# The last five output products of a fused attention and two-MLP kernel, by seven products of 256 columns

## The chip, the core and the metric

One core of a Trainium2 chip runs the whole program. The metric is the device time of one execution in microseconds, as a median of runs. The matrix engine is TensorE (PE in the rows, PEld for its weight loads), the vector engine VectorE (DVE), the scalar engine ScalarE (ACT); SP issues nearly all DMAs.

## The reference: what is computed

A linear attention with a normalisation gives x of 2304 tokens by 512; a first MLP with a gate follows, and then the second block, to which the change belongs:

```python
a = x @ w_a          # (2304, 512) @ (512, 1536)
b = x @ w_b          # (2304, 512) @ (512, 1536)
return (a * b @ w_out).astype(np.float32)   # (2304, 1536) @ (1536, 512)
```

## The kernel before

The matrices are kept as pairs of float32r, a high part and a low part (value minus high), and each product is three matmuls: high by high, high by low, low by high.

The tokens form six blocks of 384, and two blocks make a pair d (0, 1, 2). The 1536 hidden columns form six pairs p of 2 x 128. A *step* n (0 to 17) is one d and one p; in the middle pair of blocks (steps 6 to 11) p runs backwards. In a step TensorE computes *half a* (a = x @ w_a, transposed) and *half b*, and then the *output product of the step before*, as `out_mm(n - 1)` stands behind `products(n)` in the loop. The output of step 17 comes last.

Both halves use a seven-product scheme (function `seven`, L691 for its matmuls): two blocks by two hidden blocks, seven products of sums instead of eight plain ones. Products go to four PSUM banks X, Y, V, X, Z, V, Z; a bank that comes twice is accumulated into after its first value was read. u2 is ScalarE's copy of the first product, completed by an add (L698) behind the second; u3 is an add behind the third (L701). Then the four results A11, A22, A12, A21 (block of tokens, hidden half) fall out behind the products 3 to 6, counted from 0, of half a by a copy (L730) and adds (L732), of half b by an add (L745) and a product with a's result (L742, L746). Each result gets a high part on ScalarE (L748) and a low part on VectorE (L752), in a page `ab`.

The output product `out_mm` takes, for two blocks and three groups of 128 tokens, six matmuls of 512 columns (L885) into one of four PSUM banks of the tag `acc`, and adds the bank to the accumulator in SBUF (L893); the first step of a pair of blocks copies it on ScalarE (L891), the last one also stores it.

The weights' parts (`wa`, `wb` as seven operands, `w_out` as two tiles) lie in DRAM (`wd`, nine tiles of 512 KB per p) and are loaded by `load_pairs` (L652) as far ahead as 21 live tiles allow. They share 37 pages of SBUF with the parts of `ab`, the accumulators and temporary tiles. At the turn from one pair of blocks to the next the tiles of two p's stay (`KEPT`). In steps 7 to 10 sums of the next pair's x are made on ScalarE and VectorE between the output adds (`combine`, L437, L438, L491), and stored.

The order on each engine is the order in which the code issues instructions. An engine executes its queue in that order.

Of the kernel before, what the change touches and what calls it, by code (L numbers as in the profile page):

```python
# [15 lines left out]
P = 128  # L16
# [44 lines left out]
def tile_linattn_moe_moe2(ctx: ExitStack, tc: tile.TileContext, q, k, v, g_norm,  # L61
# [25 lines left out]
    had = dr.tile([NF1 // 2, P, 3 * DM], F32, tag="had", name="had")  # L87
    hsd = dr.tile([NF1 // 2, 2, P, 2 * DM], F32, tag="hsd", name="hsd")
    xcd = dr.tile([NB // 2, 7, P, 2, 2, TB], F32, tag="xcd", name="xcd")
    wd = dr.tile([NF2 // 2, 9, P, 2 * DM], F32, tag="wd", name="wd")  # L90
    first = tc.alloc_tile_pool(name="first", bufs=1)

    def page(shape, dt, name):
        return sb.tile(shape, dt, tag="page", bufs=NPAGE, name=name)
# [534 lines left out]
    NPAIR = NF2 // 2  # L629
    seq = [(d, p) for d in range(NB // 2) for p in (range(NPAIR) if d % 2 == 0 else reversed(range(NPAIR)))]  # L630
    live, wanted = [(0, False)] * 7, []
    for n, (d, p) in enumerate(seq):
        if n >= NPAIR and n % NPAIR < KEPT:
            continue
        end = n
        if d + 1 < NB // 2 and n % NPAIR >= NPAIR - KEPT:
            end = (d + 1) * NPAIR + NPAIR - 1 - n % NPAIR
        order = tuple(range(9)) if n >= NPAIR else (7, 8) + (tuple(range(7)) if n else ())
        wanted.extend((p, i, end) for i in order)

    def load_pairs(most=NLIVE):
        for _ in range(most):
            if not wanted or len(live) >= NLIVE:
                return
            p, i, end = wanted.pop(0)
            live.append((end, i >= 7))
            if len(w2raw) < NF2 and i >= 7:
                load_w(("w2", 2 * p + i - 7))
                w2raw.append((p, i - 7))
                continue  # L650
            t = page([P, 2 * DM], F32R, f"wp_{p}_{i}")
            nc.sync.dma_start(t.bitcast(F32), wd[p, i])  # L652
            wp[p, i] = t

    def free_pairs(n, last):

        live[:] = [e for e in live if e[0] > n or e[1] != last]
# [54 lines left out]
    def seven_ab(d, p, mat, place):  # L712
        return seven(f"{'ab'[mat]}_{d}_{p}", lambda name, wq, kt: w_part(p, mat, name, wq, kt),
                     lambda i, xq, kt: xc[d, i][:, xq, kt, :],
                     lambda nm: sb.tile([P, TB], F32, tag=place, bufs=PLACES[place], name=nm))

    PLACES = {"mid": 5, "sig": 2, "gh": 2, "gl": 2}
    ab = {}

    def products(d, p, after=None, more=()):  # L720

        a = {}
        for n, got in enumerate(seven_ab(d, p, 0, "mid")):
            if n == 2 and after is not None:
                after()
            if got is not None:
                f, i, z, u = got
                t = a[f, i] = sb.tile([P, TB], F32, tag="mid", bufs=5, name=f"a_{d}_{p}_{f}{i}")
                if u is None:
                    nc.scalar.copy(t, z)  # L730
                else:
                    nc.vector.tensor_add(t, z, u)  # L732
            if 1 <= n <= len(more):
                more[n - 1]()
        low = None
        for n, got in enumerate(seven_ab(d, p, 1, "sig")):
            if got is None:
                continue
            f, i, z, u = got
            t = a[f, i]  # L740
            if u is None:
                nc.vector.tensor_mul(t, z, t)  # L742
            else:
                c = sb.tile([P, TB], F32, tag=("gh", "gl")[f], bufs=2, name=f"b_{d}_{p}_{f}{i}")
                nc.vector.tensor_add(c, z, u)  # L745
                nc.vector.tensor_mul(t, c, t)  # L746
            o = page([P, 2, TB], F32R, f"ab_{d}_{p}_{f}{i}")
            nc.scalar.copy(o[:, 0], t)  # L748

            if low:  # L750
                low()
            low = lambda t=t, o=o: nc.vector.tensor_sub(o[:, 1], t, o[:, 0].bitcast(F32))  # L752
            ab[d, p, f, i] = o
        low()

    whole_ = {}

# [111 lines left out]
    def rows(j, t):  # L869
# [2 lines left out]
            return blk.rearrange("(p c) m -> p c m", c=CH)[:, t]  # L872
        return blk[t * P:(t + 1) * P]

    def out_mm(n, more=()):

        d, p = seq[n]
        first_, last_ = n % NPAIR == 0, n % NPAIR == NPAIR - 1
        for n in range(2):
            for i in range(CH):  # L880
                c = n * CH + i
                ts = slice(i * P, (i + 1) * P)
                o = ps.tile([P, DM], F32, tag="acc", bufs=4, name=f"op_{d}_{p}_{c}")
                for k, (f, g, wq) in enumerate([(f, g, wq) for f in range(2) for g, wq in ((0, 0), (0, 1), (1, 0))]):
                    nc.tensor.matmul(o, ab[d, p, f, n][:, g, ts], wp[p, 7 + f][:, wq * DM:(wq + 1) * DM],  # L885
                                     start=(k == 0), stop=(k == 5))
                if first_ and c % 2 == 0:
                    oacc[d, c // 2] = page([P, 2, DM], F32, f"o_{d}_{c}")
                t = oacc[d, c // 2][:, c % 2]
                if first_:  # L890
                    nc.scalar.copy(t, o)  # L891
                else:
                    nc.vector.tensor_add(t, o, t)  # L893
                if last_:
                    nc.sync.dma_start(rows(2 * d + n, i), t)
                for f in more[c] if c < len(more) else ():
                    f()
        for f in range(2):
            for n in range(2):
                ab.pop((d, p, f, n))  # L900


    w1 = [(kind, f) for f in range(NF1) for kind in ("wi", "wo")]
# [337 lines left out]
    with tc.manual_schedule():  # L1241
# [61 lines left out]
            x1s = [(vi, NF1 - 1)]  # L1303
        prev = 8, NF1 - 1
        todo, late = [], {}
        for n, (d, p) in enumerate(seq):
            new = 0 < n < NPAIR
            m = n % NPAIR
            if 1 <= m <= 4 and n < 2 * NPAIR:

                kt, h = divmod(m - 1, 2)
                if h == 0:
                    late[kt] = combine(d + 1, kt, late.pop("blocks"))
                todo = late[kt][6 * h:6 * h + 6]
            products(d, p, (lambda: x1_mm(*prev)) if n == 0 else None,
                     decode_out(p, 0) if 0 < n < NPAIR else [])
            if n % NPAIR == NPAIR - 1 and n + 1 < len(seq):
                for i in range(7):
                    load_x(d + 1, i)
            free_pairs(n, False)  # L1320
            load_pairs()
            if n > 0:
                more = [(f,) for f in decode_out(p, 1)] if new else []
                if todo:
                    more = [(tuple(more[i]) if more else ()) + tuple(todo[i]) for i in range(6)]
                out_mm(n - 1, more)
                todo = []
                free_pairs(n - 1, True)
                load_pairs()
            if n < 2 * NPAIR and m in (0, 2):  # L1330
                late["blocks"] = last_blocks(d + 1, m // 2)
            put()
# [32 lines left out]
```

## Time and profile before

| | us |
|---|---|
| median of 3 runs | 864.08 (863.89 to 864.09) |
| the profiled execution | 864.65 |
| its span | 862.9 |
| TensorE, VectorE, ScalarE busy | 852.0, 621.1, 347.2 |
| a step of the last pair of blocks | 22.79 |

The span runs from the first to the last instruction; the rest of the execution's time lies around it. Step 6 begins at 577.46, step 12 at 714.26, step 17 at 828.20, the output product of step 17 at 851.0. A row of the timeline gives the start from the span's begin, the time to the end of its last instruction, engine, line, operation, tiles (out<-in), shapes and how many instructions it merges; in brackets the idle time of the engine before it and what ended it. Matmuls overlap, so the distance of starts is what one costs.

### The profile page before, as it was taken

What the parts mean: (1) busy time and instruction counts of PE and PEld (TensorE: products, weight loads), DVE (VectorE), ACT (ScalarE), POOL (GpSimd) and SP (SyncE); (2) the same over time, 40 slices, a digit from 0 to 9 for tenths busy, and PEclk for the clock granted to TensorE, in tenths of its full rate; (3) what the DMA queues carried; (4) which work ended last, traced back from release to release, by engine and by line L of the source; (5) the groups of instructions that cost most, each with busy time, mean ns of one, the idle gap of its engine ahead of it and who ended that gap; (6) DMA issues with size and microseconds to landing.
All of it is one profiled execution on the core that took longest, in us unless ns stands there. A gap on an engine that the chain in (4) does not pass through costs nothing. (4 is left out here: it accounts for less than half of the span.)

```text
span 862.9 us, 13632 instructions
## 1 busy us (share of the span) xinstructions
PE 852.0 (99%) x4966; PEld 807.0 (94%) x4967; DVE 621.1 (72%) x1191; ACT 347.2 (40%) x708; POOL 52.7 (6%) x73
## 2 busy tenths in 40 slices
PE   8999999999999999999999999999999999999998
PEld 5799999999999999999999999999999999999996
DVE  4879979777946879797766788876576665535555
ACT  4667765544535556555532533221412211121110
POOL 5430211000000400000000000000000000000000
PEclk9999999999999999999999999999999999999999
DMA  9995876289986659998899888496788475755001
GB/s 285 356 265 166 230 241 211 92 313 405 402 298 186 207 213 372 407 394 314 314 417 416 321 331 335 147 372 236 255 291 287 141 283 205 293 220 195 1 0 74
DMA packets 126147, 226.35 MB, mean 262 GB/s; under 512 B 40704, under 2 KB 86272, under 8 KB 126080
## 3 DMA queue, kind: packets, MB, share of 16 engines
q1 hardware_dynamic: 126080, 225.48, 72.7%
q8 instruction: 39, 0.64, 0.3%
q14 instruction: 28, 0.23, 0.1%
HBM read 156.50 MB, written 68.94 MB: 261 GB/s over the span
## 5 line engine op out<-in xcount | busy, mean ns | idle before, releaser
L380 PE MATMUL x1p<-gh,wo 128*128 128x384 f32 x768 | 194.9, 337 | 0.0
L380 PEld LDWEIGHTS x1p<-gh,wo 128*128 128x128 f32 x768 | 138.0, 188 | 0.3 <-ACT gh L364 0.3
L380 PE MATMUL x1p<-gl,wo 128*128 128x384 f32 x384 | 128.4, 338 | 0.8 <-DVE gl L369 0.8
L885 PE MATMUL op<-wp,ab 128*128 128x512 f32 x360 | 83.4, 390 | 0.0
L748 ACT CAST ab<-a 128x384 fp32r<-128x384 f32 x72 | 37.0, 514 | 115.1 <-DVE a L742 58.2
L885 PEld LDWEIGHTS op<-wp,ab 128*128 128x128 f32 x360 | 67.5, 188 | 13.7
L369 DVE TENSOR_TENSOR gl<-g,gh 128x384 fp32r<-128x384 f32 x96 | 54.0, 564 | 31.6 <-ACT gh L364 31.3
L380 PEld LDWEIGHTS x1p<-gl,wo 128*128 128x128 f32 x384 | 71.9, 188 | 2.8 <-DVE gl L369 2.6
L893 DVE TENSOR_TENSOR o<-op,o 128x512 f32<-128x512 f32 x90 | 60.3, 684 | 16.7 <-PE op L885 16.7
L885 PE MATMUL op<-w,ab 128*128 128x512 f32 x288 | 66.9, 390 | 0.0
L885 PEld LDWEIGHTS op<-w,ab 128*128 128x128 f32 x288 | 54.0, 188 | 10.9
L364 ACT CAST gh<-g 128x384 fp32r<-128x384 f32 x96 | 49.1, 512 | 21.9 <-PE x1p L380 18.6
L354 PE MATMUL hp<-xh,wi 128*128 128x384 f32 x256 | 52.7, 345 | 0.4 <-ACT xh L260 0.3
L238 POOL TENSOR_TENSOR rr<-ss,nhalf 128x6 f32<-128x6 f32 x24 | 34.4, 1435 | 229.8 <-DVE ss L233 229.8
L354 PEld LDWEIGHTS hp<-xh,wi 128*128 128x128 f32 x256 | 43.8, 188 | 1.4 <-ACT xh L260 1.0
L691 PE MATMUL Z_a<-xc,wp 128*128 128x384 f32 x216 | 43.4, 335 | 0.1
L691 PE MATMUL Z_b<-xc,wp 128*128 128x384 f32 x216 | 43.3, 335 | 0.0
L691 PE MATMUL V_b<-xc,wp 128*128 128x384 f32 x216 | 43.3, 335 | 0.0
L691 PE MATMUL V_a<-xc,wp 128*128 128x384 f32 x216 | 43.3, 335 | 0.0
L752 DVE TENSOR_TENSOR ab<-a,ab 128x384 fp32r<-128x384 f32 x72 | 39.8, 553 | 2.3 <-ACT ab L748 0.8
L691 PE MATMUL X_a<-xc,wp 128*128 128x384 f32 x204 | 41.3, 337 | 0.0
L691 PE MATMUL X_b<-xc,wp 128*128 128x384 f32 x204 | 40.9, 334 | 0.0
(175 smaller groups left out, 1555.2 us busy)
## 6 DMA issues: line engine op xcount, KB each, us to landing
wp<-wd SPq DMA_DIRECT2D x107, 512.0 KB, 6.2
hw<-hsd SPq DMA_DIRECT2D x32, 512.0 KB, 8.3
xc<-xcd SPq DMA_DIRECT2D x21, 768.0 KB, 8.5
hw<-had SPq DMA_DIRECT2D x16, 768.0 KB, 8.4
xcd<-b SPq DMA_DIRECT2D x24, 384.0 KB, 4.5
raw_wi<-in_moe_w_in_dram SPq DMA_DIRECT2D x16, 512.0 KB, 6.6
raw_wo<-in_moe_w_out_dram SPq DMA_DIRECT2D x16, 512.0 KB, 6.2
hsd<-hs SPq DMA_DIRECT2D x16, 512.0 KB, 5.3
```

What stands on the lines that cost most here:

```text
L238: nc.gpsimd.tensor_tensor(r, rms[j, p], nhalf, op=ALU.pow)
L354: nc.tensor.matmul(o, w[wp][:, kt * P:(kt + 1) * P], x[key][:, kt, :], start=(n == 0), stop=(n == 3 * KD - 1))
L364: nc.scalar.copy(gh, src)
L369: nc.vector.tensor_sub(gl, src, gh.bitcast(F32))
L380: nc.tensor.matmul(acc[vi][c], w[wp][:, c * P:(c + 1) * P], gg[vi, s][g], start=(s == s0 and i == 0), stop=(s == s1 - 1 and i == 2))
L691: nc.tensor.matmul(b[bank], w(name, wq, kt), x(i, xq, kt), start=(fresh and k == 0), stop=(k == 5), skip_group_check=True)
L748: nc.scalar.copy(o[:, 0], t)
L752: low = lambda t=t, o=o: nc.vector.tensor_sub(o[:, 1], t, o[:, 0].bitcast(F32))
L885: nc.tensor.matmul(o, ab[d, p, f, n][:, g, ts], wp[p, 7 + f][:, wq * DM:(wq + 1) * DM], start=(k == 0), stop=(k == 5))
L893: nc.vector.tensor_add(t, o, t)
```

## The change

The output products of steps 12 to 16 are made from a 2 x 2 form as well: blocks of tokens by hidden halves on one side, the hidden halves by 256 output columns of `w_out` on the other. Seven products of 256 columns each (three groups of tokens, three matmuls each: 63 matmuls) replace 36 matmuls of 512 columns (`out_seven`). Their partial results are accumulated in two pairs of banks, U and Z, and are read out after each product: 512 columns (two token groups) and 256 columns (the third).

For that, half b of those steps ends in sums: S1 = A21 + A22 behind its last product, and S2, S3, S4 in the next half a, behind its products 1 and 2, with the low parts spread over the products behind; the low parts of S3 and A12 lie in the output product behind its products 1 and 2. A21 itself gets no parts. In steps 12 to 16 the output product of the step before stands between half a and half b, instead of behind b; in step 17 it stands behind b as before.

The sums T1 to T4 of `w_out` are made in half a of steps 8 to 12 (`t_parts`) from the tiles of the step before. The sums of steps 7, 8 and 9 are stored as two more tiles each in `wd` and loaded again; those of steps 10 and 11 stay. From step 6 to step 11 the tiles ahead are limited to 17, then to 21 again, plus the four kept T tiles. The diff, cut:

```diff
+    def by_seven(n):
+        return 2 * NPAIR <= n < 3 * NPAIR - 1
...
         order = tuple(range(9)) if n >= NPAIR else (7, 8) + (tuple(range(7)) if n else ())
+        if by_seven(n):
+            order += 9, 10
...
-    def load_pairs(most=NLIVE):
+    nlive, more_live = [NLIVE], []
+    def load_pairs(most=2 * NLIVE):
         for _ in range(most):
-            if not wanted or len(live) >= NLIVE:
+            if not wanted or len(live) >= nlive[0] + sum(more_live):
...
-                     lambda nm: sb.tile([P, TB], F32, tag=place, bufs=PLACES[place], name=nm))
-
-    PLACES = {"mid": 5, "sig": 2, "gh": 2, "gl": 2}
+                     lambda nm: sb.tile([P, TB], F32, tag=place if isinstance(place, str) else place[nm[:2]],
+                                        bufs=5 if place == "mid" else 2, name=nm))
...
+    def a_half(d, p, after=None, more=(), place="mid"):
 
         a = {}
-        for n, got in enumerate(seven_ab(d, p, 0, "mid")):
+        for n, got in enumerate(seven_ab(d, p, 0, place)):
...
-                more[n - 1]()
-        low = None
+                for fn in more[n - 1]:
+                    fn()
+        return a
...
+    def b_half(d, p, a, sums_too=False):
+        low = {}
+        def high(name, t):
+            o = ab[d, p, name] = page([P, 2, TB], F32R, f"ab_{d}_{p}_{name}")
+            nc.scalar.copy(o[:, 0], t)
+            low[name] = lambda: nc.vector.tensor_sub(o[:, 1], t, o[:, 0].bitcast(F32))
+        st = {}
...
+            name = f"A{i + 1}{f + 1}"
+            st[name] = t
+            if sums_too:
+                if name != "A21":
+                    high(name, t)
+                continue
+            wait = list(low)
+            high(name, t)
+            for e in wait:
+                low.pop(e)()
+        if not sums_too:
+            low.pop("A21")()
+            return [], []
+        def sub(op, to, x, y, tag):
+            t = st[to] = sb.tile([P, TB], F32, tag=tag, bufs=2, name=f"{to}_{d}_{p}")
+            op(t, st[x], st[y])
+            high(to, t)
+        def lo(name):
+            return lambda: low.pop(name)()
+        sub(nc.vector.tensor_add, "S1", "A21", "A22", "gh")
+        return ([(lambda: sub(nc.vector.tensor_sub, "S2", "S1", "A11", "gl"),
+                  lambda: sub(nc.vector.tensor_sub, "S3", "A11", "A21", "sig")),
+                 (lo("S1"), lambda: sub(nc.vector.tensor_sub, "S4", "A12", "S2", "sig")),
+                 (lo("A11"),), (lo("S2"), lo("A22")), (lo("S4"),), ()],
+                {1: lo("S3"), 2: lo("A12")})
...
+    H2 = 2 * P
+    OUT_PRODUCTS = (("A11", "B11", "U", ((0, 0),)), ("S1", "T1", "Z", ((1, 1),)), ("S2", "T2", "U", ((0, 1),)),
+                    ("S4", "B22", "Z", ((0, 1),)), ("S3", "T3", "U", ((1, 1),)), ("A12", "B21", "W", ((0, 0),)),
+                    ("A22", "T4", "U", ((1, 0),)))
...
+    def out_seven(n, more):
+        d, p = seq[n]
+        first_ = n % NPAIR == 0
+        banks_ = {c: [ps.tile([P, 2, H2], F32, tag="acc", bufs=4, name=f"{c}o{i}_{d}_{p}") for i in range(2)]
+                  for c in "UZ"}
+        banks_["W"] = banks_["Z"]
+        begun, done = set(), set()
+        for m, (an, bn, bank, outs) in enumerate(OUT_PRODUCTS):
+            x = ab[d, p, an]
+            if bn[0] == "B":
+                w, c0, step = wp[p, 6 + int(bn[1])], (int(bn[2]) - 1) * H2, DM
+            else:
+                e = int(bn[1]) - 1
+                w, c0, step = wp[p, 9 + e // 2], e % 2 * H2, DM
+            for i in range(CH):
+                o = banks_[bank][i // 2]
+                for k, (xq, wq) in enumerate(((0, 0), (0, 1), (1, 0))):
+                    fresh = (bank, i // 2) not in begun
+                    begun.add((bank, i // 2))
+                    nc.tensor.matmul(o[:, i % 2], x[:, xq, i * P:(i + 1) * P], w[:, wq * step + c0:wq * step + c0 + H2],
+                                     start=fresh, stop=(k == 2), skip_group_check=True)
+                if i == 0:
+                    continue
+                for r, h in outs:
+                    hs = slice(h * H2, (h + 1) * H2)
+                    t, e = o_at(d, r, 0 if i == 1 else 2, first_)
+                    t, z = (t[:, :, hs], o) if i == 1 else (t[:, e, hs], o[:, 0])
+                    if first_ and (r, h, i) not in done:
+                        nc.scalar.copy(t, z)
+                    else:
+                        nc.vector.tensor_add(t, z, t)
+                    done.add((r, h, i))
+            if m in more:
+                more.pop(m)()
...
+    def t_parts(n):
+        d, p = seq[n]
+        keep = n >= 2 * NPAIR - KEPT
+        tmp, o = [], []
+        def whole(f):
+            if f == 0:
+                t = page([P, 2, DM], F32, f"wf_{p}")
+                tmp.extend((t[:, 0], t[:, 1]))
+            w = wp[p, 7 + f].bitcast(F32)
+            nc.vector.tensor_add(tmp[f], w[:, 0:DM], w[:, DM:])
+        def first_two():
+            t = page([P, 4, H2], F32, f"t_{p}")
+            tmp.append(t)
+            nc.vector.tensor_sub(t[:, 0], tmp[0][:, H2:], tmp[0][:, 0:H2])
+            nc.vector.tensor_sub(t[:, 2], tmp[1][:, H2:], tmp[0][:, H2:])
+        def last_two():
+            t = tmp[2]
+            nc.vector.tensor_sub(t[:, 1], tmp[1][:, H2:], t[:, 0])
+            nc.vector.tensor_sub(t[:, 3], tmp[1][:, 0:H2], t[:, 1])
+        def high():
+            for i in range(2):
+                o.append(page([P, 2 * DM], F32R, f"wt_{p}_{i}"))
+                nc.scalar.copy(o[i][:, 0:DM], tmp[2][:, 2 * i:2 * i + 2].rearrange("p i f -> p (i f)"))
+        def low():
+            for i in range(2):
+                nc.vector.tensor_sub(o[i][:, DM:], tmp[2][:, 2 * i:2 * i + 2].rearrange("p i f -> p (i f)"),
+                                     o[i][:, 0:DM].bitcast(F32))
+                if keep:
+                    wp[p, 9 + i] = o[i]
+                    live.append((4 * NPAIR - 1 - n, True))
+                else:
+                    stores.append(lambda i=i: nc.sync.dma_start(wd[p, 9 + i], o[i].bitcast(F32)))
+            if keep:
+                more_live.append(2)
+        return [(lambda: whole(0),), (lambda: whole(1),), (first_two,), (last_two,), (high,), (low,)]
...
+        chain, later = [], {}
+        def out_step(n, more=(), later=()):
+            if by_seven(n):
+                out_seven(n, later)
+            else:
+                out_mm(n, more)
+            free_pairs(n, True)
+            load_pairs()
...
-            products(d, p, (lambda: x1_mm(*prev)) if n == 0 else None,
-                     decode_out(p, 0) if 0 < n < NPAIR else [])
+            more = [(f,) for f in decode_out(p, 0)] if new else chain
+            if NPAIR < n - 1 < 2 * NPAIR:
+                more = t_parts(n - 1)
+            a = a_half(d, p, (lambda: x1_mm(*prev)) if n == 0 else None, more,
+                       {"u2": "gh", "u3": "gl"} if by_seven(n - 1) else "mid")
+            swap = 2 * NPAIR <= n < len(seq) - 1
+            if swap:
+                out_step(n - 1, (), later)
+            for e in sorted(later):
+                later.pop(e)()
+            after_b = b_half(d, p, a, by_seven(n))
+            if swap:
+                chain, later = after_b
+            if n in (NPAIR, 2 * NPAIR - 1):
+                nlive[0] = 17 if n == NPAIR else NLIVE
...
-            if n > 0:
+            if n > 0 and not swap:
                 more = [(f,) for f in decode_out(p, 1)] if new else []
                 if todo:
                     more = [(tuple(more[i]) if more else ()) + tuple(todo[i]) for i in range(6)]
-                out_mm(n - 1, more)
+                out_step(n - 1, more, later)
                 todo = []
-                free_pairs(n - 1, True)
-                load_pairs()
```

## Rows read from the trace of the kernel before

**Rows 1.** The page: busy time (share) and instructions, and the span in 40 slices.
```profile
PE 852.0 (99%) x4966; PEld 807.0 (94%) x4967; DVE 621.1 (72%) x1191; ACT 347.2 (40%) x708; POOL 52.7 (6%) x73
...
PEclk9999999999999999999999999999999999999999
```

**Rows 2.** Timeline of TensorE over step 15: half a's first products, the output product.
```profile
782.62 1.23 PE L691 MATMUL X_a<-xc,wp 128*128 128x384 f32 x6
783.69 1.20 PE L691 MATMUL Y_a<-xc,wp 128*128 128x384 f32 x6
784.73 1.20 PE L691 MATMUL V_a<-xc,wp 128*128 128x384 f32 x6
...
797.21 8.36 PE L885 MATMUL op<-wp,ab 128*128 128x512 f32 x36
```

**Rows 3.** The chain that ended last: start, us on the chain, step.
```profile
797.37 8.20 PE op L885 x36
```

**Rows 4.** Stretches of steps 8, 10, 13, 15: us, PE, PEld, DVE, ACT, POOL, clock, DMA, GB/s.
```profile
623.06:645.86 22.80, 22.80 (x121) 21.36 (x120) 14.34 (x27) 5.42 (x11) 0.00 (x0) 1.00 0.82 291
...
668.66:691.46 22.80, 22.80 (x121) 21.36 (x120) 15.94 (x31) 4.55 (x10) 0.00 (x0) 1.00 0.42 143
...
737.05:759.84 22.79, 22.79 (x122) 21.35 (x121) 10.28 (x19) 6.23 (x12) 0.00 (x0) 1.00 0.68 254
...
782.62:805.41 22.79, 22.79 (x122) 21.35 (x120) 13.46 (x24) 3.50 (x7) 0.00 (x0) 1.00 0.44 162
```

**Rows 5.** Groups by shape: count, busy us, mean ns of one, idle before.
```profile
L885 PEld LDWEIGHTS op<-wp,ab 128*128 128x128 f32 x360 | 67.5, 188 | 13.7
...
L893 DVE TENSOR_TENSOR o<-op,o 128x512 f32<-128x512 f32 x90 | 60.3, 684 | 16.7 <-PE op L885 16.7
...
L791 DVE TENSOR_TENSOR hs<-hs 128x512 fp32r<-128x512 f32 x16 | 10.3, 683 | 0.6 <-ACT hs L787 0.6
...
L256 PE MATMUL xtp<-ident,sq 128*128 128x128 f32 x48 | 7.8, 272 | 0.0
```

**Rows 6.** Timeline of weight loads after a wait: one load, then two, in windows.
```profile
538.02 0.19 PEld L691 LDWEIGHTS Z_a<-xc,wp 128*128 128x128 f32 x1 [0.44 <-DVE a L732]
...
538.02 0.30 PEld L691 LDWEIGHTS Z_a<-xc,wp 128*128 128x128 f32 x2 [0.44 <-DVE a L732]
```

**Rows 7.** Timeline of TensorE: three transposes; the product behind the one that waited.
```profile
304.29 0.49 PE L256 MATMUL xtp<-ident,sq 128*128 128x128 f32 x3
...
539.17 0.51 PE L691 MATMUL X_b<-xc,wp 128*128 128x384 f32 x2
```

**Rows 8.** Timeline of VectorE: two sums of 256 columns; the add that was waited for.
```profile
103.37 0.42 DVE L781 TENSOR_TENSOR hs<-hs,hs 128x256 f32<-128x256 f32 x1
103.71 0.42 DVE L782 TENSOR_TENSOR hs<-hs 128x256 f32<-128x256 f32 x1
...
537.42 0.55 DVE L732 TENSOR_TENSOR a<-Z_a,u_a 128x384 f32<-128x384 f32 x1
```

**Rows 9.** Timeline of VectorE in step 15: A22's add, b's tail, output adds.
```profile
788.05 0.56 DVE L732 TENSOR_TENSOR a<-Z_a,u_a 128x384 f32<-128x384 f32 x1 [1.52 <-PE Z_a L691]
...
797.93 0.55 DVE L752 TENSOR_TENSOR ab<-a,ab 128x384 fp32r<-128x384 f32 x1
798.40 0.55 DVE L745 TENSOR_TENSOR b<-Z_b,u_b 128x384 f32<-128x384 f32 x1
798.98 0.56 DVE L746 TENSOR_TENSOR a<-b,a 128x384 f32<-128x384 f32 x1
...
800.60 1.88 DVE L893 TENSOR_TENSOR o<-op,o 128x512 f32<-128x512 f32 x3
```

**Rows 10.** Timeline of ScalarE in step 15: u2's copy, a high part.
```profile
783.88 0.48 ACT L696 COPY u_a<-X_a 128x384 f32<-128x384 f32 x1 [6.58 <-PE X_a L691]
...
799.57 0.52 ACT L748 CAST ab<-a 128x384 fp32r<-128x384 f32 x1 [1.01 <-DVE a L746]
```

**Rows 11.** Timeline of SP: issues of weight loads in step 7.
```profile
604.46 18.44 SPq L652 DMA_DIRECT2D wp<-wd  x9
```

More of the change, by code (lines that the diff above doesn't have):

```diff
@@ L89, in tile_linattn_moe_moe2 @@
     xcd = dr.tile([NB // 2, 7, P, 2, 2, TB], F32, tag="xcd", name="xcd")
-    wd = dr.tile([NF2 // 2, 9, P, 2 * DM], F32, tag="wd", name="wd")
+    wd = dr.tile([NF2 // 2, 11, P, 2 * DM], F32, tag="wd", name="wd")
     first = tc.alloc_tile_pool(name="first", bufs=1)
@@ L714, in seven_ab @@
                      lambda i, xq, kt: xc[d, i][:, xq, kt, :],
-                     lambda nm: sb.tile([P, TB], F32, tag=place, bufs=PLACES[place], name=nm))
-    PLACES = {"mid": 5, "sig": 2, "gh": 2, "gl": 2}
+                     lambda nm: sb.tile([P, TB], F32, tag=place if isinstance(place, str) else place[nm[:2]],
+                                        bufs=5 if place == "mid" else 2, name=nm))
     ab = {}
-    def products(d, p, after=None, more=()):
+    def a_half(d, p, after=None, more=(), place="mid"):
         a = {}
-        for n, got in enumerate(seven_ab(d, p, 0, "mid")):
+        for n, got in enumerate(seven_ab(d, p, 0, place)):
             if n == 2 and after is not None:
@@ L746, in products @@
                 nc.vector.tensor_mul(t, c, t)
[L747 to L754, printed above, removed]
+            name = f"A{i + 1}{f + 1}"
[23 more added lines that the diff above has]
+                {1: lo("S3"), 2: lo("A12")})
     whole_ = {}
@@ L873, in rows, with o_at @@
         return blk[t * P:(t + 1) * P]
+    def o_at(d, n, i, first_):
+        k, e = (n, i) if i < 2 else (2, n)
+        if first_ and (d, k) not in oacc:
+            oacc[d, k] = page([P, 2, DM], F32, f"o_{d}_{k}")
+        return oacc[d, k], e
     def out_mm(n, more=()):
@@ L884, in out_mm @@
                 for k, (f, g, wq) in enumerate([(f, g, wq) for f in range(2) for g, wq in ((0, 0), (0, 1), (1, 0))]):
-                    nc.tensor.matmul(o, ab[d, p, f, n][:, g, ts], wp[p, 7 + f][:, wq * DM:(wq + 1) * DM],
+                    nc.tensor.matmul(o, ab[d, p, f"A{n + 1}{f + 1}"][:, g, ts], wp[p, 7 + f][:, wq * DM:(wq + 1) * DM],
                                      start=(k == 0), stop=(k == 5))
-                if first_ and c % 2 == 0:
-                    oacc[d, c // 2] = page([P, 2, DM], F32, f"o_{d}_{c}")
-                t = oacc[d, c // 2][:, c % 2]
+                t, e = o_at(d, n, i, first_)
+                t = t[:, e]
                 if first_:
@@ L897, in out_mm @@
                     f()
-        for f in range(2):
-            for n in range(2):
-                ab.pop((d, p, f, n))
+        for name in ("A11", "A12", "A21", "A22"):
+            ab.pop((d, p, name))
+    H2 = 2 * P
+    OUT_PRODUCTS = (("A11", "B11", "U", ((0, 0),)), ("S1", "T1", "Z", ((1, 1),)), ("S2", "T2", "U", ((0, 1),)),
+                    ("S4", "B22", "Z", ((0, 1),)), ("S3", "T3", "U", ((1, 1),)), ("A12", "B21", "W", ((0, 0),)),
+                    ("A22", "T4", "U", ((1, 0),)))
@@ new lines, in out_seven @@
+    def out_seven(n, more):
[32 more added lines that the diff above has]
+                more.pop(m)()
+        for name in ("A11", "A12", "A22", "S1", "S2", "S3", "S4"):
+            ab.pop((d, p, name))
```

## Prediction

> **What bounds the kernel now.** I read the page's busy line and its slices first: TensorE is busy 99% of the span at the full granted clock, VectorE 72%, ScalarE 40% [rows 1]. The core has one bottleneck, and only two things can move the end: fewer microseconds of matmuls, or a wait that TensorE doesn't have today. Then I read the chain of work that ended last and TensorE's timeline over one step of the last pair of blocks. A step is a half a (7 products of 6 matmuls), a half b (the same) and one output product of 36 matmuls, each beginning where the one before it ends [rows 2, 3]. A product of the halves takes 1.04 us (0.173 per matmul of 384 columns), the output product 8.20 us (0.228 per matmul of 512 columns); 14 x 1.04 + 8.20 is the 22.79 us of a step in the stretches [rows 4]. In those stretches VectorE works 10.3 to 15.9 us of 22.8: it has room, but the question is where in the step.
>
> **What the change takes from TensorE.** Five output products (steps 12 to 16) go from 36 matmuls of 512 columns to 63 of 256. No row has 256 columns, so the pitch is worked out. 384 columns at 2.4 GHz are 160 ns and take 173, 512 are 213 and take 228: 13 to 14 ns beside the columns. For 256 that is 107 + 13 = 120 ns, so 63 x 0.120 = 7.56 us and a gain of 8.20 - 7.56 = 0.64 us per product, 3.2 us in all. Bounds: each matmul has its own weight load, shown as 188 ns [rows 5], more than the pitch would be. But where TensorE starts again after a wait, two such loads stand 0.11 us apart (0.30 - 0.19) [rows 6], and transposes of 128 columns, a load each, follow one another in (0.49 - 0.27)/2 = 0.11 us [rows 5, 7]; so 0.108 is the low end. The high end is the nearest row of the same form, 0.173. I take 0.120, which lies on the line through the two rows of the form.
>
> Here a rule of the Trainium skill is to be weighed ("TensorE: Matmul & The Clock Gate", Back-to-back issue gap): a matmul stream is spaced by its columns at 2.4 GHz and 2.5 ns. By it 256 columns would take 109 ns. The trace disagrees: by the rule 384 columns would take 162 ns, and the rows have 173.
>
> **What a wait costs.** Where TensorE did wait for VectorE on a bank, VectorE's add of 0.55 us began at 537.42, the load began at 538.02, 0.05 us after its end, and the next product began at 539.17, 1.15 us later instead of 1.04: the first load is no longer hidden [rows 6 to 8]. So TensorE can begin 0.16 us after the add's end, not earlier.
>
> **What the change adds to VectorE.** Durations on the timeline are longer than the distance at which independent operations follow one another: 0.47 us for 384 columns, 0.60 for 512 (1.88 - 0.68 over two), 0.33 for 256, and about 0.12 more behind an operation whose result is read [rows 8, 9]. An add of 512 columns takes 684 ns from PSUM and 683 between SBUF tiles [rows 5], so the 256-column rows, all of SBUF, stand for PSUM too. Per step of seven products: 7 x (0.60 + 0.33) = 6.5 us of output adds instead of 6 x 0.60 = 3.6, and four sums and three more low parts, 7 x 0.47 = 3.3. That is 6.2 us more beside about 13 us of work, some 19 in 22: it fits by the sum, and so the order decides. I lay VectorE's queue in the order of the code against TensorE's products. Laid so for the kernel before, the same distances meet the trace within 0.1 us.
>
> *Half a, steps 13 to 17* (0 is its start). Before, VectorE adds A22 at 788.05 - 782.62 = 5.43, ends at 5.99, and TensorE may reuse that bank at 6.15, where it wants it at 6.24: 0.09 us to spare [rows 9]. In the new order, the tail of b is A21's add at 0.22, its product at 0.80, and S1, which reads that product, from 1.38 to 1.93. ScalarE has S1's high part (0.51) ahead of the copy of u2 in its queue, so that copy, which ended at 784.36 - 782.62 = 1.74, now ends at about 2.9 [rows 10]. u2's add begins at 2.93, and then come S2 3.40, S3 3.87, u3 4.33, S1 low 4.80, S4 5.27, A11 low 5.73, and only then A22's add, 6.20 to 6.75. TensorE goes on at 6.91 instead of 6.24: 0.67 us, five times, 3.4 us. The sums stand behind the adds of their own product, but ahead of the next one's.
>
> *Output product, steps 13 to 16.* It starts at 7.95; VectorE is done with half a at 9.0. Its adds take 0.93 us per product against 9 x 0.120 = 1.08, but two low parts (0.94) stand among them, so the add behind product 3 ends at 13.45 and the bank for product 5 is free at 13.61, where it is wanted at 13.35: 0.26 us. In step 13 most first additions are ScalarE copies and this doesn't occur: three times, 0.8 us.
>
> *The last steps.* In step 17 half b stands directly ahead of the output product of step 16. There VectorE's tail is in the trace: the output starts at 797.21 and the first output add at 800.60, 3.39 us later [rows 2, 9]. Before, four banks cover this (4 x 1.37 us). Now the bank of product 0 is wanted again by product 2, at 2.16 us; its add ends at 3.39 + 0.68 = 4.07, with 0.16 that is 4.23: a wait of 2.0 us. And the output of step 17 wants the same bank at the end of product 6, where its add is still to be made: 0.7 us.
>
> *Edits costed at nothing.* The sums of w_out2 (steps 8 to 12): 4 operations of 512 and 4 of 256 columns, about 3.9 us of VectorE, in half a; idle there are 22.8 - 15.9 = 6.9 us per step at the fullest [rows 4]. Laid out, T1 and T4 end near 5.2, ahead of A22's 5.43; without that cover each 0.1 us late is 0.1 us of TensorE. The two ScalarE copies lie behind A11's copy, with 4.6 to 5.4 us of its work per step [rows 4]. Stores: six of 512 KB on SP at the end of steps 8 to 10, behind loads that already wait there; six more loads in the last pair, at DMA shares of 0.42 to 0.82 per step. 17 tiles ahead instead of 21: the nine loads issued at 604.46 to 622.90 would then be three of step 8 and six of step 9 [rows 11]; the first that step 8 needs, in half b, is used at 623.06 + 7.28 + 2.08 = 632.4. The out-before-b order at step 12 moves work without adding any. The cost of pages that come free later can't be read from this trace; its bound is nothing to one load's way, about 6 us.
>
> Sum: -3.2 + 3.4 + 0.8 + 2.0 + 0.7 = +3.7 us. On the profiled execution (864.65 with its span of 862.9) that is 868.3, on the median of 864.08 it is **867.8 us**.
>
> **Rivals.** *The vector queue isn't late* (the other side): if A22's add ends by 6.08 and product 0's add in the last output by 2.0, TensorE keeps its 3.2 us and the time is 860.9. For it: VectorE has some 3 us of slack per step by the sum. Against it: the laid queue misses the first point by 0.67 us and the last by 2.0, and that last tail is in the rows. With the first point kept and only the last steps' 2.7 us paid, it is 863.6.
>
> *A pitch at the load's own distance*: 0.1085 gives 5 x (8.20 - 6.84) = -6.8, but then VectorE sets the pace of the output product and the waits grow to 8.5: +1.7, 865.8. The Trainium skill's 109 ns, above, would be this case.
>
> *Loads not hidden at 256 columns*: at 0.140 the products take 8.8 us, VectorE's waits shrink, and the steps grow by some 1.2 to 1.4 us: 873. At 0.173 it is 10.9 us per product and 883. The busy line of weight loads (94%) [rows 1] speaks for it, the 0.11 us between loads against. The Trainium skill has a rule that speaks for it ("TensorE: Matmul & The Clock Gate", The mechanism): a load overlaps matmuls only in other row groups. The trace disagrees: loads of 188 ns and matmuls of whole arrays share a pitch of 173.
>
> *Pages*: a VectorE sum that waits for a page behind a store holds the adds behind it, and then TensorE: 869 to 873.
>
> **How the numbers follow.** Chances: forecast 0.56 (its own range 865.7 to 869.5); queue not late, nothing paid 0.12; only the last steps paid 0.08; pitch at the load's distance 0.12; loads not hidden 0.08; pages 0.04. Differences under 0.2% (1.7 us) can't be told from no change by a measurement of this kernel. Faster 0.12; within it 0.22 (863.6, 865.8 and 0.02 of the forecast's low edge); slower 0.66. The range takes in all but the full gain and the unhidden loads: 863.2 to 871.2.
>
> **What would show it.** Right: TensorE's output stretch of steps 12 to 15 near 7.6 to 7.8 us; idle time ahead of the second Z product of half a, about 0.7 us, released by VectorE's add of A22; one wait of about 2 us early in the output product of step 16; VectorE busy 18 us or more per step. Wrong: a pitch other than 0.120, no idle time of TensorE, or idle time in steps 6 to 11.

## The result, and the profile after

| | before | changed |
|---|---|---|
| median of 6 runs each on one chip, us | 863.99 (863.74 to 864.25) | 868.34 (866.97 to 869.84) |
| ratio, 95% interval | | 1.0051 (1.0039 to 1.0064) |
| profiled execution, us | 864.65 | 869.37 |
| its span, us | 862.9 | 867.6 |

The change makes the kernel 4.35 us slower; 867.8 was forecast. The page of the changed kernel, busy time and granted clock, against [rows 1]:

```profile
PE 852.3 (98%) x5102; PEld 812.3 (94%) x5102; DVE 668.5 (77%) x1304; ACT 359.8 (41%) x735; POOL 52.7 (6%) x73
...
PEclk9999999999999999999999999999999999999998
```

TensorE is busy for as long as before (852.3 and 852.0 us) although five output products were to take 3.2 us less. The last slice of the clock has an 8. Stretches of steps 8, 10, 13, 15 and 17 (the last from its half a to the output product that ends the kernel), columns as in [rows 4]:

```profile
623.06:645.86 22.80, 22.80 (x122) 21.36 (x121) 17.95 (x35) 6.57 (x13) 0.00 (x0) 1.00 0.68 255
668.65:691.46 22.81, 22.81 (x122) 21.36 (x121) 19.66 (x39) 5.70 (x12) 0.00 (x0) 1.00 0.52 189
737.06:759.88 22.82, 22.43 (x148) 22.11 (x148) 15.56 (x32) 8.18 (x18) 0.00 (x0) 1.00 0.88 346
782.93:805.98 23.05, 22.66 (x148) 22.16 (x148) 19.08 (x40) 4.79 (x10) 0.00 (x0) 1.00 0.66 229
829.03:855.39 26.36, 24.15 (x148) 23.62 (x148) 21.88 (x45) 5.81 (x12) 0.00 (x0) 0.94 0.00 1
```

Steps 8 and 10 are as long as before, with 3.6 and 3.7 us more VectorE work in them: the sums of w_out2 are hidden. Step 13 is where it was, step 15 0.26 us longer, step 17 3.6 us longer, and in these three TensorE is no longer busy throughout. TensorE's timeline over step 15, against [rows 2]:

```profile
788.17 1.20 PE L699 MATMUL V_a<-xc,wp 128*128 128x384 f32 x6
789.76 1.31 PE L699 MATMUL Z_a<-xc,wp 128*128 128x384 f32 x6 [0.39 <-DVE a L740]
790.91 1.24 PE L972 MATMUL Uo<-wp,ab_A 128*128 128x256 f32 x9
791.99 1.24 PE L972 MATMUL Zo<-wp,ab_S 128*128 128x256 f32 x9
...
795.23 1.24 PE L972 MATMUL Uo<-wp,ab_S 128*128 128x256 f32 x9
796.45 1.34 PE L972 MATMUL Zo<-wp,ab_A 128*128 128x256 f32 x9
```

Nine matmuls of 256 columns follow one another in 791.99 - 790.91 = 1.08 us: the pitch is 0.120. The second Z product of half a begins 1.59 us behind V_a instead of 1.04, and the product behind it 1.15 later: 0.66 us lost. Product 5 of the output begins 1.22 behind product 4 instead of 1.08. Why the Z product waits, on ScalarE and then VectorE, against [rows 9, 10]:

```profile
784.95 0.51 ACT L752 CAST ab_S<-S 128x384 fp32r<-128x384 f32 x1 [1.14 <-DVE S L783]
785.37 0.47 ACT L704 COPY u_a<-X_a 128x384 f32<-128x384 f32 x1
```

```profile
784.36 0.56 DVE L783 TENSOR_TENSOR S<-a,a 128x384 f32<-128x384 f32 x1
785.87 0.56 DVE L706 TENSOR_TENSOR u_a<-Y_a,u_a 128x384 f32<-128x384 f32 x1 [0.96 <-ACT u_a L704]
...
789.15 0.55 DVE L740 TENSOR_TENSOR a<-Z_a,u_a 128x384 f32<-128x384 f32 x1
```

ScalarE makes S1's high part before u2's copy; VectorE stands idle for 0.96 us for that copy, begins u2's add 2.94 us into half a and, behind six more operations, A22's add at 6.22 (before: 5.43). All waits of TensorE from step 6 on, by what it waited for (us in total, times, longest):

```profile
PE Z_a L699 <- DVE a L740: 2.0, 5, 0.4
PE Uo L972 <- DVE o L983: 1.8, 1, 1.8
```

No wait for a load is among them. The end, on TensorE's timeline, and the same stretch by single microseconds (columns as in [rows 4]):

```profile
848.41 1.68 PE L972 MATMUL Uo<-wp,ab_S 128*128 128x256 f32 x9 [1.82 <-DVE o L983]
849.89 2.12 PE L972 MATMUL Zo<-wp,ab_S 128*128 128x256 f32 x9
851.81 1.59 PE L972 MATMUL Uo<-wp,ab_S 128*128 128x256 f32 x9
853.24 1.24 PE L972 MATMUL Zo<-wp,ab_A 128*128 128x256 f32 x9
```

```profile
848.00:849.00 1.00, 0.59 (x5) 0.59 (x6) 1.00 (x3) 0.00 (x0) 0.00 (x0) 1.00 0.00 0
849.00:850.00 1.00, 1.00 (x8) 1.00 (x7) 1.00 (x3) 0.00 (x0) 0.00 (x0) 0.59 0.00 0
850.00:851.00 1.00, 1.00 (x7) 1.00 (x7) 0.56 (x2) 0.00 (x0) 0.00 (x0) 0.50 0.00 0
```

Product 2 waits 1.82 us for its bank. Behind the wait the granted clock goes to its lower level, 0.50 or 1.2 GHz, and products 2 to 4 take 1.48, 1.92 and 1.43 us; in a second profile of this kernel, at full clock (below), they take 1.17, 1.08 and 1.08. That is another 1.5 us, which no step of the prediction has.

### The profile page after: what moved, and what is told of

The parts are those of the page before. It is cut to its first block, busy times and chain, and to the rows that moved or that the text cites. A ratio compares the mean times of both kernels' runs of the same rounds, so it can differ in the third digit from the quotient of the medians.

```text
span 867.6 us, 14093 instructions
## 1 busy us (share of the span) xinstructions
PE 852.3 (98%) x5102; PEld 812.3 (94%) x5102; DVE 668.5 (77%) x1304; ACT 359.8 (41%) x735; POOL 52.7 (6%) x73
## 5 line engine op out<-in xcount | busy, mean ns | idle before, releaser
L752 ACT CAST ab_A<-a 128x384 fp32r<-128x384 f32 x67 | 34.4, 514 | 107.6 <-DVE a L762 58.2
L932 PE MATMUL op<-w,ab_A 128*128 128x512 f32 x288 | 66.9, 390 | 0.0
L932 PEld LDWEIGHTS op<-w,ab_A 128*128 128x128 f32 x288 | 53.9, 188 | 10.9
L939 DVE TENSOR_TENSOR o<-op,o 128x512 f32<-128x512 f32 x66 | 44.8, 685 | 11.0 <-PE op L932 11.0
L932 PE MATMUL op<-wp,ab_A 128*128 128x512 f32 x180 | 41.8, 390 | 0.0
L699 PEld LDWEIGHTS Z_a<-xc,wp 128*128 128x128 f32 x216 | 37.7, 188 | 4.0 <-DVE a L740 4.0
L932 PEld LDWEIGHTS op<-wp,ab_A 128*128 128x128 f32 x180 | 33.7, 188 | 6.8
```

What stands on the lines that cost most here:

```text
L699: nc.tensor.matmul(b[bank], w(name, wq, kt), x(i, xq, kt), start=(fresh and k == 0), stop=(k == 5), skip_group_check=True)
L932: nc.tensor.matmul(o, ab[d, p, f"A{n + 1}{f + 1}"][:, g, ts], wp[p, 7 + f][:, wq * DM:(wq + 1) * DM], start=(k == 0), stop=(k == 5))
```

## The experiments

The theory that the prediction left: TensorE's 0.64 us per product is real, and VectorE and ScalarE, in the order in which their queues are written, give it back at three places (the second Z product, product 5's bank, product 2's bank in step 16's output). The median of the kernel before differs by up to 1 us from chip to chip, so each time stands beside the kernel before on its own chip. Step lengths below are distances between starts on TensorE's timeline.

**One operation moved.** (x1_s1_high_later) S1's high part issued behind u2's copy:

```
-            high(to, t)
+            if to != "S1":
+                high(to, t)
...
-        return ([(lambda: sub(nc.vector.tensor_sub, "S2", "S1", "A11", "gl"),
+        return ([(lambda: high("S1", st["S1"]), lambda: sub(nc.vector.tensor_sub, "S2", "S1", "A11", "gl"),
```

> One order on ScalarE is changed in the changed kernel: the high part of S1 is issued behind the copy of u2 of the next half a, not ahead of it. Theory (the order decides): u2's copy no longer waits for S1, u2's add begins at 2.3 us of half a instead of 2.9, A22's add ends 0.6 us earlier, and the wait of 0.65 us ahead of the second Z product is gone in all five steps: 868.3 - 5 x 0.65 = 865.1 us, steps 14 to 16 at 22.4 us instead of 23.05; the wait of step 17 in the output product and what follows it stay. Rival (the amount of VectorE's work decides): the same work in the same stretch gives the same 868.3 us, with the wait in another place.

Measured: 864.88 us (863.94 to 868.20) against 864.84, ratio 1.0003 (0.9993 to 1.0012). Step 13 takes 22.24 us, steps 14 to 16 take 22.46 to 22.47. TensorE's timeline of step 17, the Z product and the product that waits in the output:

```profile
831.95 1.31 PE L699 MATMUL Z_a<-xc,wp 128*128 128x384 f32 x6
...
844.52 1.34 PE L973 MATMUL Uo<-wp,ab_S 128*128 128x256 f32 x9 [1.82 <-DVE o L984]
```

The Z product begins 1.04 behind its forerunner; only its first load is still exposed (1.31, and 1.15 to the next product). One place in ScalarE's queue was thus worth 0.57 to 0.59 us a step, five times, with the same work on VectorE. The wait of 1.82 is as before.

**The last product left as it was.** (x2_four_products) Step 16 with 36 matmuls of 512 columns:

```
-        return 2 * NPAIR <= n < 3 * NPAIR - 1
+        return 2 * NPAIR <= n < 3 * NPAIR - 2
```

> The output product of step 16 goes back to 36 matmuls of 512 columns; steps 12 to 15 stay at seven products. Theory (the fall of the granted clock in step 17 follows the wait of 1.8 us idle in its output product, and that wait follows from the bank of product 0 being wanted again by product 2): no such wait, the clock stays at full, and what is left is 0.03 us in step 13 and 0.26 us in each of the steps 14 to 16: 864.0 + 0.8 = 864.8 us. Rival (the clock falls because of 63 narrow matmuls with their loads, not because of the wait): the clock falls in the steps before and the time stays above 866 us.

Measured: 865.74 us, ratio 1.0008 (1.0000 to 1.0017). No wait of 1.8 is left, and four of 0.4 instead of five; steps 13 to 16 take 22.83, 23.04, 23.07 and 23.07. So 0.9 us of the change's cost belongs to four products. The rest, 1.5 us of the 2.4 measured for the changed kernel below and 3.5 of the 4.35 above, belongs to the fifth, forecast as -0.64 + 0.67 + 2.0 + 0.7 (the 0.67 in half a of step 17; there the plain half b of step 16 leaves another wait of 0.28, as in the next experiment but one).

**The wait filled.** (x3_filled_wait) Nine matmuls of 512 columns, whose result nobody reads, between products 1 and 2 of step 16's output:

```
+            if m == 1 and n == len(seq) - 2:
+                idle = ps.tile([P, DM], F32, tag="h", bufs=2, name="idle")
+                for _ in range(9):
+                    nc.tensor.matmul(idle, ab[d, p, "A11"][:, 0, 0:P], wp[p, 7][:, 0:DM], start=True, stop=True)
```

> Nine matmuls of 512 columns whose result nobody reads (9 x 0.228 = 2.05 us) stand in the output product of step 16 between products 1 and 2, where TensorE stands idle in the changed kernel. Theory (idleness lowers the clock): product 2 begins at about the same time, the clock stays at full, products 2 to 4 take 1.08 us each again and 1.5 us come back; of them 0.7 go to the wait for the same bank ahead of the last output product, which the slow clock had covered: 867.5 us, and runs within 0.5 us of each other instead of 2.9. Rival (the clock falls for another reason): a stretch at half clock at the same place and 868.3 us or more.

Measured: 868.03 us (867.35 to 870.52), ratio 1.0038 (1.0025 to 1.0051), on TensorE's timeline:

```profile
846.70 2.23 PE L990 MATMUL idle<-wp,ab_A 128*128 128x512 f32 x9
848.77 1.25 PE L972 MATMUL Uo<-wp,ab_S 128*128 128x256 f32 x9
849.86 1.24 PE L972 MATMUL Zo<-wp,ab_S 128*128 128x256 f32 x9
```

Behind the filler each product takes 1.08 to 1.09 us: full clock. Alone this decides nothing, for a second profile of the changed kernel (below) has full clock without a filler. The runs were to lie within 0.5 us of each other and lie 3.2 apart; the slowest has a mean clock of 0.998, and where it lost it isn't known. Nor is there a wait of 0.7 ahead of the last output product: it begins 1.08 us behind product 6.

**Everything but the seven products.** (x4_no_seven) The sums of w_out2, their stores, 17 tiles and the order "output before half b" of steps 12 to 16 stay; the output is 36 matmuls and half b the plain one:

```
-            if by_seven(n):
-                out_seven(n, later)
-            else:
-                out_mm(n, more)
+            out_mm(n, more)
...
-            after_b = b_half(d, p, a, by_seven(n))
+            after_b = b_half(d, p, a)
```

> Everything of the change but the seven products: the sums of w_out are made and stored in steps 8 to 12, their tiles loaded, 17 tiles ahead in the middle pair of blocks, the output product between the halves in steps 12 to 16, but made by 36 matmuls of 512 columns; half b makes no sums. Theory (these edits are hidden): 864.0 us, no wait of TensorE from step 6 on. Rival (pages or loads that come late): 866 to 870 us with idle time in steps 8 to 14.

Measured: 866.42 us, ratio 1.0016 (1.0008 to 1.0025): not free. Steps 6 to 11 take 22.80 each, so the sums, the stores and the 17 tiles are. But steps 13 to 16 take 23.07 to 23.10. TensorE's and ScalarE's timelines of step 14:

```profile
761.82 1.20 PE L699 MATMUL V_a<-xc,wp 128*128 128x384 f32 x6
763.04 1.31 PE L699 MATMUL X_a<-xc,wp 128*128 128x384 f32 x6
```

```profile
762.09 0.51 ACT L752 CAST ab_A<-a 128x384 fp32r<-128x384 f32 x1 [1.01 <-DVE a L766]
762.51 0.47 ACT L704 COPY u_a<-X_a 128x384 f32<-128x384 f32 x1
```

With the output between the halves, the next half a follows half b directly. ScalarE has the high part of the last product of b ahead of u2's copy, the copy ends at 762.98, and the second X product, which needs that bank, begins 1.22 us behind V_a instead of 1.04, with its first load exposed. It is the same queue and the same copy as in the first experiment, without any sum of the change.

**The last output between the halves too.** (x5_last_between) Step 17 like steps 12 to 16:

```
-            swap = 2 * NPAIR <= n < len(seq) - 1
+            swap = 2 * NPAIR <= n
```

> In step 17 too the output product of the step before stands between half a and half b. Theory: the wait of 2.0 us inside that product goes (step 17 takes 23.05 us, 3.3 less), but the last output product now stands directly behind half b and needs the low part of A12, which VectorE ends 2.9 us behind half b: a wait of 2.9 us there, and the clock falls behind it, some 1.7 us more: 868.3 - 3.3 + 2.9 + 1.7 = 869.6 us. Rival (only the bank was the matter): 865.0 us.

Measured: 867.11 us (867.07 to 867.26) against 864.28, ratio 1.0034 (1.0022 to 1.0047). Step 17 up to the end of its half b takes 23.08 us and the wait of 1.8 is gone, but TensorE's timeline of the last output product has two others:

```profile
852.86 0.73 PE L932 MATMUL op<-wp,ab_A 128*128 128x512 f32 x2 [0.55 <-ACT ab_A L752]
854.31 7.33 PE L932 MATMUL op<-wp,ab_A 128*128 128x512 f32 x31 [0.72 <-DVE ab_A L753]
```

Now it is this product that stands directly behind half b. It asks for A12's high part 0.68 us after b's end (three matmuls) and for its low part behind that, before VectorE's tail has them. Five matmuls (1.14 us) take 854.31 - 851.46 = 2.85: 1.71 us in the place of 2.0, where a wait of 2.9 and a fall of the clock were expected; the clock stays at full. The wait has moved, and the time is where the changed kernel is without the fall of the clock (below).

**All three.** (x6_all_three) The two moves above, and in the last output product the matmuls with high parts ahead of those with low parts:

```
+        for c in range(4):
+            mm(c, False)
+        for c in range(4):
+            mm(c, True)
+            read(c)
```

> Three edits together: S1's high part behind u2's copy, the output product between the halves in step 17 too, and in the last output product the matmuls that need high parts of a*b alone first for four banks (16 x 0.228 = 3.6 us), the ones with low parts behind. Theory: no wait ahead of the second Z product (step 13 at 22.15 us, steps 14 to 17 at 22.4 with 0.26 us of the bank wait left), none in the last output product, full clock throughout: 864.0 - 0.6 - 4 x 0.37 = 861.9 us, ratio to the kernel before 0.9976, faster than both. Rival (VectorE's work, some 19 us of 22, decides): waits move to other places and the time stays at or above 864.

Measured: 863.34 us against 864.28, ratio 0.9990 (0.9981 to 0.9999); 861.9 was expected. Steps 14 to 16 take 22.46 to 22.48, so the bank wait of product 5 is still in each, as expected. Not expected was a wait of 0.77 us in the last output for A12's high part, since the first group of tokens asked for it behind only two matmuls.

**An order in which nothing waits.** (x8_no_wait_left) Worked out beforehand by laying the three queues against one another with the distances of the prediction. Low parts of A11, A22 and A12 inside half b; S1's high part as above; S2, S4, S3 one to a product of half a; the last output in the order in which its operands are ready, which is 36 matmuls as before; the output of step 17 between the halves:

```
+                done = {"A22": "A11", "A12": "A22", "A21": "A12"}.get(name)
+                if done:
+                    low.pop(done)()
...
+        return ([(lambda: high("S1", st["S1"]), lambda: sub(nc.vector.tensor_sub, "S2", "S1", "A11", "gl")),
+                 (lambda: sub(nc.vector.tensor_sub, "S4", "A12", "S2", "sig"),),
+                 (lambda: sub(nc.vector.tensor_sub, "S3", "A11", "A21", "sig"),),
+                 (lo("S1"), lo("S2")), (lo("S4"),), ()],
+                {1: lo("S3")})
```

> An order of the same additions laid out so that no product waits: the low parts of A11, A22 and A12 are made inside half b, S1's high part behind u2's copy, S2, S4, S3 one to a product of the next half a; the output of steps 12 to 17 all lie between the halves; the last output takes its products in the order in which A11, A22, A12 and A21 are ready. Nothing of the computation is left out. Theory of the queues (each wait is set by what stands ahead on VectorE or ScalarE, and goes when the queue is laid out otherwise): the waits of 0.26 before product 5, of 0.4 ahead of the second Z product, of 1.8 in the output of step 16 and of 0.7 in the last output all go, steps 13 to 17 take 22.1 to 22.2 us against 22.46 in x6_all_three, and the whole is 3 us below the kernel before on the same chip, ratio 0.9965 (0.9955 to 0.9975). Rival: the waits are a matter of VectorE's load as a whole in these steps, so that a wait taken from one place comes up at another; then steps 13 to 17 stay at 22.45 and the ratio stays at 0.999. Second rival: the 256-column product is slower for another reason beside its pitch; then no wait is seen and steps take over 22.3.

Measured: 861.27 us (861.09 to 861.69) against 864.95, ratio 0.9957 (0.9944 to 0.9971). Stretches of steps 13, 15 and 17:

```profile
737.03:759.15 22.12, 22.12 (x148) 22.09 (x148) 15.39 (x32) 8.29 (x18) 0.00 (x0) 1.00 0.93 351
781.29:803.42 22.13, 22.13 (x148) 22.09 (x148) 19.06 (x40) 4.84 (x10) 0.00 (x0) 1.00 0.70 239
825.55:847.69 22.14, 22.14 (x149) 22.10 (x148) 19.07 (x40) 4.84 (x10) 0.00 (x0) 1.00 0.01 1
```

TensorE is busy throughout, with the same 19.1 us of VectorE work in a step as the changed kernel. The load of VectorE was never the matter; its order, with ScalarE's, was. This kernel is 3.7 us faster than the kernel before on the same chip. How much of the step from 22.46 to 22.13 us belongs to which of its moves was not measured.

**The changed kernel again, beside it.** (x9_changed_again)

> The changed kernel once more, unaltered, beside x8_no_wait_left on one chip. Theory: the fall of the granted clock behind the 1.8 us without a matmul in step 16's output happens in some runs only, so the time lies between 866.5 (no fall) and 870 (fall) where the kernel before takes 864.0 to 864.8, ratio 1.003 to 1.006. Rival: the fall came from the one chip of the first measurement and is not seen here; then all runs lie within 0.3 us of 867.0 and the profile shows clock 1.00 in every stretch of 1 us behind the wait.

Measured: 867.39 us (866.86 to 868.09), ratio 1.0030 (1.0018 to 1.0043). Its TensorE timeline at the end, and VectorE's last operation of the seven products:

```profile
847.89 1.34 PE L972 MATMUL Uo<-wp,ab_S 128*128 128x256 f32 x9 [1.82 <-DVE o L983]
849.06 1.24 PE L972 MATMUL Zo<-wp,ab_S 128*128 128x256 f32 x9
...
853.38 8.35 PE L932 MATMUL op<-wp,ab_A 128*128 128x512 f32 x36
```

```profile
853.22 1.02 DVE L983 TENSOR_TENSOR o<-Uo,o 128x512 f32<-128x512 f32 x2
```

The same wait to the hundredth, and no fall of the clock behind it: from product 2 to the last output it is 5.49 us instead of 6.98. The mean clock is 0.999 or 1.000 in all five runs, so the rival, that the fall belongs to the chip of the first measurement, is not refuted by this experiment.

**The wait made longer.** (x10_wait_of_4, x11_wait_of_6) To see whether the fall belongs to the wait, idle additions on VectorE ahead of the first output addition of step 16, four and eight:

```
+            for _ in range(4):
+                nc.vector.tensor_add(sb.tile([P, TB], F32, tag="gl", bufs=2, name="more"), x, x)
```

> The changed kernel with four idle additions of 384 columns on VectorE ahead of the first output addition of step 16, each 0.47 us behind the other, so that TensorE's wait in the last seven-product output grows from 1.8 to 3.7 us. Theory (the fall of the granted clock in the first profile of the changed kernel came from TensorE's time without a matmul, and a longer one brings it each time): the clock is 0.5 for about 3.4 us behind the wait, which gives back another 1.5 us; beside x9_changed_again, 867.4 with a wait of 1.8 and full clock, this is 867.4 + 1.9 + 1.5 = 870.8. Rival (the fall has nothing to do with the wait): clock 1.00 behind it and 867.4 + 1.9 = 869.3.

> The same with eight idle additions, so that the wait is 5.6 us. Theory: half clock for 3.4 us or longer behind it in every run, 867.4 + 3.8 + 1.5 = 872.7 or more. Rival: full clock, 871.2. If the fall shows here and not in x10_wait_of_4, the length of the wait from which it comes surely lies between 3.7 and 5.6 us, and 1.8 is a length at which it comes in some runs only.

Measured: 871.03 us (870.79 to 871.83) and 873.85 us (872.66 to 874.74) against 864.63. Half clock for 3.4 us takes 0.002 off a run's mean granted clock. That mean was 0.996 to 0.998 in all four runs with four additions and 0.995 to 0.996 in all four with eight. The kernel before has 0.998 or less in one run of seven beside them, and in 7 of all 61 runs beside the experiments, so the mean alone does not tell where in a run a fall lies; the profiles do. TensorE's timeline and stretches with four:

```profile
850.02 2.29 PE L976 MATMUL Uo<-wp,ab_S 128*128 128x256 f32 x9 [3.88 <-DVE o L987]
```

```profile
849.00:850.00 1.00, 0.00 (x0) 0.00 (x0) 0.90 (x3) 0.00 (x0) 0.00 (x0) 0.89 0.00 0
850.00:851.00 1.00, 0.98 (x4) 0.98 (x5) 1.00 (x3) 0.00 (x0) 0.00 (x0) 0.50 0.00 0
```

and TensorE's timeline with eight:

```profile
852.70 2.29 PE L976 MATMUL Uo<-wp,ab_S 128*128 128x256 f32 x9 [5.76 <-DVE o L987]
854.79 2.12 PE L976 MATMUL Zo<-wp,ab_S 128*128 128x256 f32 x9
856.71 2.07 PE L976 MATMUL Uo<-wp,ab_S 128*128 128x256 f32 x9
```

The fall comes with the idle time: in both profiles at 3.88 and 5.76 us, and by the means in every other run of these kernels, against one of two profiles of the changed kernel at 1.82 us, whose means are 0.997 in three of the first six runs and 0.999 or 1.000 in the other eight. From product 2 to the last output it costs 6.89 - 5.49 = 1.40 us with four and 8.07 - 5.49 = 2.58 us with eight. For the wait of 1.82 us the means of all runs on record say a little more: 0.998 or less in 7 of 22 runs of the kernels that have it (changed kernel 3 of 11, x1_s1_high_later 4 of 11), and in 8 of 110 of those that have neither it nor a longer one (kernel before 7 of 61, x3_filled_wait 1 of 6, the others none of 43). That speaks for the wait and against the first chip alone, but it is a count and not a sight of each fall.

## Why the prediction was right, and where it was off

Starts of half a on TensorE's timeline give the steps (us; the last row ends at the output product of step 17):

| | before | changed | changed, again | nothing waits |
|---|---|---|---|---|
| step 12 | 22.79 | 22.81 | 22.80 | 22.80 |
| step 13 | 22.79 | 22.82 | 22.83 | 22.12 |
| steps 14 to 16, each | 22.79 | 23.05 | 23.06 | 22.13 |
| step 17 | 22.78 | 26.36 | 24.89 | 22.14 |
| all six against before | | +4.4 | +3.0 | -3.3 |

**The pitch** of 0.120 and with it 0.64 us per product was right; the kernel in which nothing waits shows the 3.2 us whole. Both rivals on the pitch fall, 0.1085 as well as 0.140 and more. By the Trainium skill's rule that a load overlaps matmuls only in other row groups ("TensorE: Matmul & The Clock Gate", The mechanism) these loads would have been in the open; the trace disagrees, with loads shown as 188 to 192 ns under a pitch of 120. That section of the Trainium skill also names a load into the background weight buffer as one that may run ahead; the trace is in keeping with that, though no run here shows which buffer a load goes to. The 109 ns that the prediction weighs is given by the Trainium skill, in the section that it names, for a matmul apart from its load; here each has one.

**A22's add**: forecast at 6.20 us into half a, found at 6.22; 0.67 us forecast, 0.66 found, five times. The chain from S1's high part over u2's copy was the cause: taking that one operation out of it gave 0.59 us a step back; the exposed first load, 0.11, stayed.

**Product 5's bank**: forecast 0.26 in steps 14 to 16 and none in step 13. That makes steps 14 to 16 longer by 0.67 + 0.26 - 0.64 = 0.29 and step 13 by 0.03; found 0.26 and 0.03. The wait itself is a little smaller than forecast: products 5 and 6 begin 1.22 and 1.17 us behind their forerunners instead of 1.08, 0.23 in all.

**The last steps**: 2.0 us forecast for product 2 of step 16's output; in the second profile it begins 847.89 - 844.82 = 3.07 behind product 1 instead of 1.08, so 1.99. The 0.7 behind it was wrong: the last output begins 1.08 behind product 6, while the additions that read product 6 begin only at 853.22 and end after its start. Since two uses of one bank would have to follow one another, the first bank of the last output isn't one that these additions read. That it wants the same bank was the step that failed; which bank it gets instead no run shows. The step's other terms stand.

**What was missing**: the fall of the clock behind the wait, 1.5 us in the first profile and none in the second. Forecast without the 0.7 was +3.0 for the six steps; +3.0 is what the second profile has, +4.4 the first. Another 0.3 us lies between the last addition and the end of the span in the three later profiles of this table; it was not looked into. So that 867.8 came this near to 868.34 is in part luck: a term too many and a term too few offset each other. In the first measurement the three runs with a mean clock of 0.997 took 868.51 to 869.84 us, the other three 866.97 to 868.16.

**Edits costed at nothing**: sums, stores and 17 tiles were free, steps 6 to 11 being as before. The order "output before half b" was said to move work without adding any. Step 12 (22.81) can't show its price, since its half a still stands behind an output product; from step 13 on half a stands directly behind half b, and with the plain half b that costs 0.28 us a step. The prediction had laid the queue for the new half b alone, where S1's high part stands at this place and the price is part of the 0.67; that the order costs by itself, it did not see.

**The rival "vector queue not late"** had 860.9 as its time. It needed another order of the same work, and with that the chip gives 861.27, where the kernel before takes 864.95.

## What to carry to other kernels

Where one engine is busy all the time, work added to another one is priced by the place in its queue at which the busy engine's next bank is released, not by its slack: 19 us of VectorE in 22 were free in one order (-3.3 us over six steps) and cost 6.3 us in another (+3.0). Lay out the in-order queues of both helping engines with measured start-to-start distances before writing the order, look first for a copy that frees a bank and for what stands ahead of it, and repeat this wherever a stage is moved, since its old neighbours meet. An output product that directly follows the stage that makes its operands should take them in the order in which they become ready.

## What the runs showed of the hardware

- TensorE's granted clock falls to half behind idle time of TensorE, also deep in a kernel that has been busy for 800 us. Behind 1.82 us it fell in one profiled execution out of three with that wait, behind 3.88 and 5.76 us in both. It stayed at half (0.50) for some 3.4, 3.4 and 6.8 us (summed from stretches of 1 us), with TensorE busy for most or all of it. In the execution with 1.82 us it fell 0.8 us after TensorE had begun again, in the other two some 0.2 and 0.9 us before. What decides between fall and no fall at 1.82 us stays open.
- A float32r matmul of 256 columns with a load of its own has a pitch of 120 ns, 13 ns more than its columns take at 2.4 GHz; those of 384 and 512 have 13 and 15 ns (173 and 228).
